# A rational feed-forward layer behind masked attention: the second matrix multiplication wholly in float16 parts, steps of 2048 columns, weights decoded two tiles at once, and another order of the last batch

## The chip, the cores and the metric

The kernel runs on one core of one Trainium2 chip. The metric is device time in microseconds (us), the median of the runs. A core has a matrix engine (TensorE, PE in the profile, with its weight loads as PEld), a vector engine (VectorE, DVE), a scalar engine (ScalarE, ACT), GpSimd (POOL) and a queue engine (SyncE, SP). Each runs its own instructions in the order in which they stand in the program, and they wait for each other by semaphores. GpSimd also issues many of the transfers, so its queue holds both arithmetic and transfers.

## The reference

Attention over 8 batches, 8 heads, 576 positions and 64 dimensions per head, in which only scores within `tau` of the row's maximum count. Its output, 4608 rows of 512, goes through a layer with 2048 hidden units, whose non-linearity is a ratio of polynomials:

```python
scores = scale * np.matmul(q, k.transpose(0, 1, 3, 2))
thresh = np.max(scores, axis=-1, keepdims=True) - tau
scores = np.where(scores >= thresh, scores, -1000000000.0)
scores = scores - np.max(scores, axis=-1, keepdims=True)
attn = np.exp(scores)
attn = attn / (np.sum(attn, axis=-1, keepdims=True) + 1e-09)
x = np.matmul(attn, v)                       # heads side by side: (4608, 512)
h = x @ w_in                                 # (512, 2048)
h2 = h * h
h3 = h2 * h
P = a[0] + a[1] * h + a[2] * h2 + a[3] * h3
Q = 1.0 + np.abs(b[0]) * np.abs(h) + np.abs(b[1]) * h2
g = P / (Q + 1e-06)
out = g @ w_out                              # (2048, 512)
```

The weights come as 64-bit words and are decoded to float32 on the chip.

## The kernel before

**Attention.** A unit is one pair of heads and one block of 128 query rows (four blocks and a rest of 64 rows; 160 units). Its scores go to three PSUM banks (L811 and L815; L804 for a rest), VectorE takes the maxima (L821, L823), ScalarE applies threshold and exponential (L836, L840), and the probabilities are split into a high float16 part, `hi` (L324 on ScalarE or L326 on VectorE), and a low one, which VectorE computes in L862 as probability times factor minus high part. A transfer transposes them and L933 multiplies them by V. The first batch goes another way, with transposes on TensorE (L885, L890, L916).

**The layer.** A chunk is 256 rows of x; there are 18 (two per batch, and two that gather the rests of four batches). The hidden units are 16 blocks of 128, called f. A step of the layer takes one chunk and four f, that is 1024 columns of a tile with 128 partitions. Per step:

- the first multiplication, L1050, in three float16 products (high by high, low by high, high by low), 12 multiplications of 256 columns for each f;
- ScalarE brings the result to a tile `t` (L1059);
- the ratio: |h| (L1064 on ScalarE or L1066 on VectorE), then on VectorE L1070, L1073, L1083, L1086, L1089 and L1092, each reading two inputs, with ScalarE's logarithm and exponential (L1077, L1080) in the middle for the reciprocal;
- the second multiplication by `w_out`. For three f of four (`PARTS`), g is split into a rounded part (L316 on ScalarE or L318 on VectorE, 256 columns each) and a remainder (L1100 on VectorE), both in the format fp32r, and L1109 makes three products of 512 columns. For the fourth f, L1113 multiplies in full float32, which the profile records as two instructions each;
- L1123 or L1118 takes the sum out of PSUM, and it is stored.

**Weights.** Each tile of 128 by 512 is loaded by GpSimd's queue, decoded by ScalarE and VectorE (L491, L497, L501, L331), and split. The scale of `w_in` comes from its largest absolute value (L543, L545 and `scale_ops`), four tiles at a time. GpSimd paces its loads with a small read of an earlier one (L481).

**The order.** No instruction is placed by hand. A planner, `Plan.order()`, simulates the engines while the program is built: every operation has a key (an aim in units of attention), a duration, what it waits for and which buffers it holds, and operations that two engines could do (`FLEX`) go to the one the planner finds sooner. The tables `WHEN`, `FLEX`, `START`, `PRICE` and `TOL` steer it. All batches go through the pairs of heads in one manner (`visits`): first half of the rows for three pairs, all rows of the fourth, then the second half and the rests on the way back. The last three chunks (`LAST`) come behind the last unit.

Of the kernel before, what the change touches and what calls it, by code (L numbers as in the profile page):

```python
# [26 lines left out]
POOLS = {"e": 3, "hi": 2, "pT": 2, "st": 8, "sc": 2, "t": 8, "u": 3, "g": 2, "x": 3, "xr": 1}  # L27
# [16 lines left out]
LAST = (0, 1, 2)
SOON = 1

# [10 lines left out]
PARTS = 3  # L57

# [27 lines left out]

TOL = {"PE": 0.1187, "ACT": 0.1137, "DVE": 0.0398, "POOL": 0.1, "DMA": 0, "GD": 0}
# [30 lines left out]
class Plan:  # L118
# [156 lines left out]
def masked_attention_rational_ffn(  # L275
# [54 lines left out]
    def tensor_tensor(dst, x, y, how):  # L330
# [28 lines left out]
    ones = bass.AP(one.tensor, one.offset, [list(one.ap[0]), [0, P]])  # L359

# [47 lines left out]
    co = op("DVE", 2.1, 6.0, monic, [co])  # L408

    def scale_ops(key, get, up, inv, s, after, ahead=0.0):  # L410
# [20 lines left out]
        def f3():  # L431
            p2 = box["p2"]
            nc.vector.tensor_reduce(box["m2"], box["all"], AX.X, ALU.max)
            nc.vector.tensor_single_scalar(p2.bitcast(I32), box["m2"].bitcast(I32), 0x7F800000, ALU.bitwise_and)
# [8 lines left out]
        return op("DVE", 0.68, key, f3, [o], (), [h, hb])  # L443
# [22 lines left out]
    def decode_ops(i, key, load, hold, dst=None):  # L466
# [4 lines left out]
        ht = Hold("u", 1)  # L471

        def ld():
# [8 lines left out]
            box["rw"] = load()  # L482
            loaded.append((box["rw"], plan.now))

        def f1():


            box["w"] = place(ht)
            w, words_ = box["w"], box["rw"][:, :, 1].bitcast(F32)
            if plan.eng == "ACT":  # L490
                nc.scalar.activation(w, words_, AF.Prelu, scale=REBIAS, alpha=SIGN)  # L491
# [11 lines left out]
        def f6():  # L503
            t = box["w"].bitcast(I32)
            if dst is None:
                tensor_tensor(box["rw"][:, :, 1], t, box["rw"][:, :, 0], ALU.add)
                box["w"] = box["rw"][:, :, 1].bitcast(F32)
            else:
                tensor_tensor(dst.bitcast(I32), t, box["rw"][:, :, 0], ALU.add)

        l = op("GD", 2.5, key - 2.0, ld, (), [hold])
        if i < NC:
            first_loads.append(l)
        o1 = op(FLEX["f1"], 0, key, f1, [l], [ht])
        o2 = op("ACT", 0.568, key, f2, [l])
        o4 = op("DVE", 0.335, key, f4, [o1])
        o6 = op(FLEX["f6"], 0, key, f6, [o4, o2], (), [ht] if dst is None else [ht, hold])
        return o6, box

# [4 lines left out]
    wm = const.tile([P, NW * NC], F32, name="wm")  # L524
# [771 lines left out]
```

## Time and profile before

| | |
|---|---|
| median of three runs | 1289.99 us (1289.88 to 1293.14) |
| profiled execution, span from first to last instruction | 1287.8 us |
| its own time with what lies around the span | not recorded apart; the fastest run is 2.1 us above the span |
| TensorE busy | 1254.2 us, 97% |
| VectorE busy | 1210.6 us, 94% |
| ScalarE busy | 1072.6 us, 83% |
| GpSimd busy | 229.4 us, 18% |
| mean granted TensorE clock | 0.995 |

Busy time is the union of an engine's instructions. On VectorE an independent successor begins some 0.08 us before its predecessor's recorded end, so what an instruction adds is the distance between two starts. On TensorE the chain of work that ended last shows what a group of multiplications takes.

### The profile page before, as it was taken

What the parts mean: (1) busy time and instruction counts of PE and PEld (TensorE: products, weight loads), DVE (VectorE), ACT (ScalarE), POOL (GpSimd) and SP (SyncE); (2) the same over time, 40 slices, a digit from 0 to 9 for tenths busy, and PEclk for the clock granted to TensorE, in tenths of its full rate; (3) what the DMA queues carried; (4) which work ended last, traced back from release to release, by engine and by line L of the source; (5) the groups of instructions that cost most, each with busy time, mean ns of one, the idle gap of its engine ahead of it and who ended that gap; (6) DMA issues with size and microseconds to landing.
All of it is one profiled execution on the core that took longest, in us unless ns stands there. A gap on an engine that the chain in (4) does not pass through costs nothing.

```text
span 1287.8 us, 25167 instructions
## 1 busy us (share of the span) xinstructions
PE 1254.2 (97%) x9296; PEld 899.3 (70%) x9296; DVE 1210.6 (94%) x1970; ACT 1072.6 (83%) x2166; POOL 229.4 (18%) x478
## 2 busy tenths in 40 slices
PE   8898999999999999999999999999999999999998
PEld 6666677677667776766777676677677677677775
DVE  5999899999999999999999999999999999998876
ACT  6988899899988888888888798888887988885454
POOL 2201000123122321232112231322122220200000
PEclk8999999999999999999999999999999999999999
DMA  8544355588567654878644775776566745542000
GB/s 243 159 124 142 117 98 102 111 149 168 93 121 142 132 111 100 124 139 122 110 86 102 130 139 108 154 130 139 94 116 132 135 101 96 110 96 29 17 17 17
DMA packets 338123, 146.64 MB, mean 114 GB/s; under 512 B 314416, under 2 KB 320720, under 8 KB 338000
## 3 DMA queue, kind: packets, MB, share of 16 engines
q1 hardware_dynamic: 316240, 87.14, 39.3%
q0 software_dynamic: 21440, 57.30, 16.5%
q8 instruction: 73, 1.20, 0.4%
q10 hardware_dynamic: 320, 0.59, 0.2%
q14 instruction: 50, 0.41, 0.1%
HBM read 60.30 MB, written 9.44 MB: 54 GB/s over the span
## 4 chain that ended last, share of the span: by engine, by line
PE 62%; DVE 17%; ACT 3%; issue 3%; DMA 2%; POOL 0%; DVEq 0%; ACTq 0%
PE banks L1050 20%; PE banks L1109 18%; PE banks L1113 8%; PE banks L815 7%; PE banks L933 7%; DVE e L862 3%; PE banks L804 2%; PE banks L811 2%; DVE t L1086 2%; DVE st L821 1%; DVE t L1092 1%; DVE t L1073 1%; DVE t L1089 1%; DVE t L1070 1%; DVE t L1083 1%
## 5 line engine op out<-in xcount | busy, mean ns | idle before, releaser
L1050 PEld LDWEIGHTS <-wi 128*128 128x128 f16 x3456 | 326.0, 98 | 104.8 <-issue 69.0
L1050 PE MATMUL banks<-x,wi 128*128 128x256 f16 x3072 | 363.6, 273 | 2.7 <-ACT t L1059 1.3
L1109 PE MATMUL banks<-wp,g 128*128 128x512 f32 x1296 | 357.6, 418 | 2.6 <-ACT g L316 1.7
L1109 PEld LDWEIGHTS banks<-wp,g 128*128 128x128 f32 x1296 | 235.7, 188 | 101.5 <-issue 36.8
L840 ACT ACTIVATE e<-e,cf 128x576 f32<-128x576 f32 x288 | 221.5, 775 | 0.4
L836 ACT ACTIVATE e<-banks,st 128x576 f32<-128x576 f32 x288 | 206.6, 737 | 14.7 <-DVE st L830 11.3
L862 DVE SCALAR_TENSOR_TENSOR e<-e,st,hi 128x576 f16<-128x576 f32 x252 | 205.0, 813 | 2.9 <-ACT hi L324 2.7
L821 DVE TENSOR_REDUCE st<-banks 128x2 f32<-128x1152 f32 x128 | 172.5, 1348 | 8.4 <-PE banks L815 8.0
L324 ACT ACTIVATE hi<-e,st 128x576 f16<-128x576 f32 x162 | 122.1, 770 | 47.4 <-DVE st L851 39.6
L1113 PE MATMUL banks<-wp,t 128*128 128x512 f32 x288 | 143.6, 613 | 2.8 <-DVE t L1092 2.8
L815 PE MATMUL banks<-KK,QQ 64*128 64x512 f32 x512 | 145.9, 645 | 0.0
L1059 ACT ACTIVATE t<-banks,hsc 128x512 f32<-128x512 f32 (+1 forms) x192 | 106.7, 575 | 36.3 <-PE banks L1050 35.4
L933 PEld LDWEIGHTS <-V 128*64 128x64 f16 x2520 | 104.2, 111 | 33.7 <-issue 30.5
L933 PE MATMUL banks<-pT,V 128*64 128x256 f16 (+1 forms) x2520 | 118.9, 248 | 3.8 <-DMA pT<-e 3.1
L1086 DVE SCALAR_TENSOR_TENSOR t<-t,co,t 128x1024 f32<-128x1024 f32 (+1 forms) x73 | 92.3, 1266 | 19.8 <-ACT t L1080 19.7
L316 ACT CAST g<-t 128x256 fp32r<-128x256 f32 x152 | 57.9, 402 | 45.7 <-PE banks L1109 34.7
L1077 ACT ACTIVATE t<-t,co 128x1024 f32<-128x1024 f32 (+1 forms) x73 | 82.7, 1133 | 12.8 <-DVE t L1083 12.4
L1092 DVE SCALAR_TENSOR_TENSOR t<-t,co,t 128x1024 f32<-128x1024 f32 (+1 forms) x73 | 92.4, 1266 | 0.6
L1083 DVE SCALAR_TENSOR_TENSOR t<-t,co,t 128x1024 f32<-128x1024 f32 (+1 forms) x73 | 92.4, 1266 | 0.0
L1070 DVE SCALAR_TENSOR_TENSOR t<-t,co 128x1024 f32<-128x1024 f32 (+1 forms) x73 | 92.3, 1264 | 0.0
L1073 DVE SCALAR_TENSOR_TENSOR t<-t,co 128x1024 f32<-128x1024 f32 (+1 forms) x73 | 92.3, 1264 | 0.0
L1089 DVE SCALAR_TENSOR_TENSOR t<-t,t 128x1024 f32<-128x1024 f32 (+1 forms) x73 | 88.0, 1206 | 0.7
(135 smaller groups left out, 1567.4 us busy)
## 6 DMA issues: line engine op xcount, KB each, us to landing
KK<-in_kT_dram POOLq DMA_DIRECT2D x84, 144.0 KB, 3.9
t<-in_w_in_dram POOLq DMA_DIRECT2D x16, 512.0 KB, 4.7
t<-in_w_out_dram POOLq DMA_DIRECT2D x16, 512.0 KB, 4.7
out_dram<-u POOLq DMA_DIRECT2D x26, 256.0 KB, 3.2
V<-in_v_dram POOLq DMA_DIRECT2D x24, 256.0 KB, 4.6
QQ<-in_qT_dram POOLq DMA_DIRECT2D x42, 144.0 KB, 3.0
QQ<-in_qT_dram POOLq DMA_DIRECT2D x42, 128.0 KB, 3.4
KK<-in_kT_dram SPq DMA_DIRECT2D x24, 144.0 KB, 3.0
```

Of the source, the lines that this page charges most:

```text
L324: nc.scalar.activation(dst, src, AF.Identity, scale=factor)
L815: nc.tensor.matmul(d, QQ[r, t * P:(t + 1) * P], KK[r, REM:S], **one)
L821: nc.vector.tensor_reduce(box["st"][:, 0:2], box["both"], AX.X, ALU.max, negate=True)
L836: nc.scalar.activation(ev(hh), box["s"][hh], AF.Prelu, scale=SCALE, bias=box["st"][:, 2 + hh:3 + hh], alpha=STEEP)
L840: nc.scalar.activation(e, e, AF.Exp, scale=passes, accum_out=box["st"][:, 4 + hh:5 + hh])
L862: nc.vector.scalar_tensor_tensor(box["lo"][:, c], ev(hh), box["st"][:, 6 + hh:7 + hh], box["hi"][:, c], ALU.mult, ALU.subtract)
L933: nc.tensor.matmul(dst, V[:, c * P + head * D:c * P + (head + 1) * D], rhs, start=c == 0 and n == 0, stop=c == NT and n == 2)
L1050: nc.tensor.matmul(d, wi_tile(c, f0 + j, hl), x[:, c, :], start=c == 0 and n == 0, stop=c == NC - 1 and n == 2)
L1059: nc.scalar.activation(box["h3"][:, 2 * k:2 * k + 2, sl], psv[:, :, sl], AF.Identity, scale=hsc[:, b2, g:g + 1])
L1086: nc.vector.scalar_tensor_tensor(box["q"], box["q"], qc, box["i"], ALU.add, ALU.mult)
L1109: nc.tensor.matmul(acc[tt], fr(g[:, x]), fr(wo[f][y]), start=begins and j == n == 0, stop=ends and j == nb - 1 and n == 2)
L1113: nc.tensor.matmul(acc[tt], box["r"][:, o:o + P], wo[f], start=begins and j == 0, stop=ends and j == nb - 1)
```

## The change

1. **Second multiplication.** All 16 f are done in three float16 products (L1322 in the new file). `PARTS`, the fp32r parts and the full float32 products are gone, and so is the pool `g`. `w_out` is held as a high and a low float16 part, scaled by a power of two for each half of the f.
2. **A scale from norms.** For float16, g needs a scale. For each chunk x is squared in bfloat16 (L1107 or L1109), TensorE sums the squares over a column with a matrix of ones (L1114), VectorE takes the largest sum and a rough root (L1117, `root`), GpSimd works out a bound for |g| in seven small operations (`bound`), VectorE rounds it to a power of two (`floor_ops`) and GpSimd writes the two factors (`gain`, `first_gain`). The scale of `w_in` comes from column norms too (L591, L593, L603, L607), and V's from a sum of squares in place of its maximum.
3. **Tiles of 2048 columns.** A step takes eight f (`NB`). Its elementwise work goes in pieces of 1024 columns (`PIECE`), and in whole steps (up to 2048 columns) for steps behind the last unit. A piece's g has one rounding (L341 or L343) and one remainder (L1313) for all its f. The last chunk's steps are 8, 4, 2 and 2 f (`TAIL`).
4. **Weights two tiles at once.** Loads and decoding work on 128 by 1024, in place in a tile `t`; with half as many loads the planner's order holds no pacing read any more.
5. **The last batch** goes through its rests of 64 rows first, then the first and then the second half (`ENDING`), and the last three chunks follow in that order (`LAST = (2, 0, 1)`).
6. **The planner's numbers.** All keys are now in a table `K`, and `WHEN`, `FLEX`, `START`, `PRICE`, `TOL` and the spacings have other values; the pool `t` has 7 buffers of twice the size.

```diff
-POOLS = {"e": 3, "hi": 2, "pT": 2, "st": 8, "sc": 2, "t": 8, "u": 3, "g": 2, "x": 3, "xr": 1}
+POOLS = {"e": 3, "hi": 2, "pT": 2, "st": 8, "sc": 2, "t": 7, "u": 3, "dg": 2, "x": 3, "xr": 1}
-PARTS = 3
+NB = 8
+PIECE = 2
+TAIL = (8, 4, 2, 2)
-LAST = (0, 1, 2)
+LAST = (2, 0, 1)
-PRICE = {"ACT": 0.7389, "DVE": 2.6699}
+PRICE = {"ACT": 2.362, "DVE": 1.311}
...
+    ENDING = [[half, other, rest][i] for i in LAST]
+        if bb == B - 1:
+            visits += [(v0 + i, x) for x in ENDING for i in range(NP)]
...
+        def f_norm():
+            sq = place(hq).bitcast(BF16).rearrange("p (c t) -> p c t", c=NC)
+            for c in range(NC):
+                nc.tensor.matmul(bank(hb)[:, 0:CT], ones_, sq[:, c, :], start=c == 0, stop=c == NC - 1)
+        def f_root():
+            nc.vector.tensor_reduce(w[:, 0:1], bank(hb)[:, 0:CT], AX.X, ALU.max)
+            root(w[:, 1:2], w[:, 0:1])
+    def bound(w, x, sigma):
+        m, k, p, q, hi = (w[:, i:i + 1] for i in range(2, 7))
+        g = nc.gpsimd
+        g.tensor_scalar(hi, w[:, 1:2], x, sigma, ALU.mult, ALU.mult)
+        g.tensor_scalar(m, hi, rqc, rbc, ALU.mult, ALU.min)
+        g.tensor_scalar(k, m, hi, 1.0, ALU.mult, ALU.min)
+        g.tensor_scalar(p, hi, g2, k, ALU.add, ALU.mult)
+        g.tensor_scalar(q, m, g1, g0, ALU.mult, ALU.add)
+        g.tensor_tensor(p, p, q, ALU.add)
+        g.tensor_scalar(p, p, 2.0 ** -100, 2.0 ** 100, ALU.max, ALU.min)
+    def floor_ops(w, key, after):
+            nc.vector.tensor_single_scalar(p.bitcast(I32), p.bitcast(I32), 0x7F800000, ALU.bitwise_and)
+            nc.vector.reciprocal(q, p)
...
+        span = nb // 2 if late else min(PIECE, nb // 2)
+        pieces = [(k, min(k + span, nb // 2)) for k in range(0, nb // 2, span)]
...
-        def f_gh(j):
-            copy(fr(box["g", j][:, 0]), box["r"][:, j * CT:(j + 1) * CT])
-        def f_gl(j):
-            nc.vector.tensor_tensor(fr(g[:, 1]), box["r"][:, j * CT:(j + 1) * CT], g[:, 0], ALU.subtract)
+        def f_gh(x):
+            times(g_parts(x)[0], cols("r", x), gscale)
+        def f_gl(x):
+            gh, gl = g_parts(x)
+            nc.vector.scalar_tensor_tensor(gl, cols("r", x), gscale, gh, ALU.mult, ALU.subtract)
         def f_g2(j, tt):
-            if in_parts(f):
-                for n, (x, y) in enumerate(((0, 0), (1, 0), (0, 1))):
-                    nc.tensor.matmul(acc[tt], fr(g[:, x]), fr(wo[f][y]), start=begins and j == n == 0,
-                                     stop=ends and j == nb - 1 and n == 2)
-                return
-            nc.tensor.matmul(acc[tt], box["r"][:, o:o + P], wo[f], start=begins and j == 0, stop=ends and j == nb - 1)
+            for n, (x, y) in enumerate(((0, 0), (1, 0), (0, 1))):
+                nc.tensor.matmul(acc[tt], g[x][:, o:o + P], wo_tile(f, y), start=begins and j == n == 0,
+                                 stop=ends and j == nb - 1 and n == 2)
```

**TensorE, second multiplication of one step.** `g`, `t` and `wp` are buffers, x2 counts repeats. Before, the end of a step in the last part of the program, one float32 block and the first of three fp32r blocks:

```order
L1113 MATMUL banks<-wp_154,t_70 128x512 x2
L1109 MATMUL banks<-wp_0_155,g_97 128x512 x2
L1109 MATMUL banks<-wp_1_156,g_97 128x512
L1109 MATMUL banks<-wp_0_155,g_97 128x512 x2
L1109 MATMUL banks<-wp_1_156,g_97 128x512
```

After, in float16, where the weight loads are instructions of their own:

```order
L1248 MATMUL banks<-x_97,wi 128x256
L1322 LDWEIGHTS t_68
L1322 MATMUL banks<-wp_134,t_68 128x512
L1322 LDWEIGHTS t_68
L1322 MATMUL banks<-wp_134,t_68 128x512
L1322 LDWEIGHTS t_68
L1322 MATMUL banks<-wp_134,t_68 128x512
```

One kind of product stands where two stood. Behind the scores of the last unit stand 480 of the first layer's multiplications (L1050), 216 of L1109 and 24 of L1113 before; after, 396 of L1248 and 330 of L1322, with eight of L1114.

**VectorE, in the middle of the program.** Before, with the ratio (L1070 to L1092), the remainders of g at 256 columns (L1100) and attention's low parts (L862):

```order
L1092 SCALAR_TENSOR_TENSOR t_74<-t_74,co,t_75 128x1024
L851 RECIPROCAL st_92<-st_92 128x2
L823 TENSOR_REDUCE st_93<-banks 128x1
L1100 TENSOR_TENSOR g_97<-t_74,g_97 128x256
L1100 TENSOR_TENSOR g_96<-t_74,g_96 128x256
L830 TENSOR_SCALAR st_93<-st_93,cf 128x1
L1070 SCALAR_TENSOR_TENSOR t_73<-t_68,co 128x1024
L862 SCALAR_TENSOR_TENSOR e_81<-e_81,st_92,hi_83 128x576
L1073 SCALAR_TENSOR_TENSOR t_72<-t_72,co 128x1024
L862 SCALAR_TENSOR_TENSOR e_81<-e_81,st_92,hi_83 128x576
L1100 TENSOR_TENSOR g_97<-t_74,g_97 128x256
```

After, at about the same place (L1273, L1277, L1287, L1291, L1295 and L1299 are the ratio, L932 the low parts):

```order
L1291 SCALAR_TENSOR_TENSOR t_72<-t_72,co,t_69 128x1024
L891 TENSOR_REDUCE st_91<-banks 128x2
L921 RECIPROCAL st_90<-st_90 128x2
L1295 SCALAR_TENSOR_TENSOR t_72<-t_72,t_69 128x1024
L1287 SCALAR_TENSOR_TENSOR t_71<-t_71,co,t_68 128x1024
L1299 SCALAR_TENSOR_TENSOR t_73<-t_73,co,t_72 128x1024
L932 SCALAR_TENSOR_TENSOR e_82<-e_82,st_90,hi_84 128x576
L1277 SCALAR_TENSOR_TENSOR t_70<-t_70,co 128x1024
L1313 SCALAR_TENSOR_TENSOR t_72<-t_73,gsc,t_72 128x1024
L932 SCALAR_TENSOR_TENSOR e_82<-e_82,st_90,hi_84 128x576
```

One remainder of 1024 columns (L1313) stands for three of 256, and two pieces of one step run through the ratio side by side (`t_71`, `t_72`). Over the whole program VectorE's roundings of `hi` go from 90 to 32 and ScalarE's from 162 to 220.

**GpSimd's queue, in the middle.** Before, loads of K and Q and stores follow each other:

```order
L653 DMA KK_116<-in_kT_dram 64x576
L654 DMA KK_116<-in_kT_dram 64x576
L718 MEMSET V_163 64x64 x2
L1132 DMA out_dram<-u_78 128x512
L1132 DMA out_dram<-u_76 128x512
L690 DMA V_161<-in_v_dram 128x4x128
```

After, a chunk's bound and factors (`gt`, `gsc`, `oscs` are columns of single numbers) stand between a store and the next load of Q:

```order
L1345 DMA out_dram<-u_77 128x512
L1130 TENSOR_SCALAR gt<-gt,isx,sg 128x1
L1131 TENSOR_SCALAR gt<-gt,co 128x1
L1132 TENSOR_SCALAR gt<-gt 128x1
L1133 TENSOR_SCALAR gt<-gt,co 128x1
L1134 TENSOR_SCALAR gt<-gt,co 128x1
L1135 TENSOR_TENSOR gt<-gt 128x1
L1136 TENSOR_SCALAR gt<-gt 128x1
L1176 TENSOR_SCALAR gsc<-gs,gt 128x2
L1177 TENSOR_SCALAR oscs<-gt,sg 128x1
L714 DMA QQ_115<-in_qT_dram 64x576
```

Over the program 186 such small operations are new on GpSimd, and the 11 pacing reads of L481 are gone.

More of the change, by code (lines that the diff above doesn't have):

```diff
@@ L141, in op @@
         engs = {eng: dur} if isinstance(eng, str) else eng
-        o = Op(engs, key, fn, [x for x in after if x is not None], list(take), list(drop))
+        o = Op(engs, key + self.shift, fn, [x for x in after if x is not None], list(take), list(drop))
         o.rank, o.tiling = self.rank, "ff"
@@ L504, in f6, with squares_ops, f @@
             t = box["w"].bitcast(I32)
-            if dst is None:
-                tensor_tensor(box["rw"][:, :, 1], t, box["rw"][:, :, 0], ALU.add)
-                box["w"] = box["rw"][:, :, 1].bitcast(F32)
-            else:
[L509 to L518, printed above, removed]
+            if dst is not None:
+                box["w"] = dst
+            tensor_tensor(box["w"].bitcast(I32), t, low.bitcast(I32), ALU.add)
+        l = op("GD", 3.4, key - 2.0 + K["load"], ld, (), [hold])
+        if i < NC // 2:
+            first_loads.append(l)
+        o1 = op(FLEX["f1"], 0, key + K["f1"], f1, [l])
+        o2 = op("ACT", 0.995, key + K["f2"], f2, [l])
+        o4 = op("DVE", 0.6, key + K["f4"], f4, [o1])
+        o6 = op(FLEX["f6"], 0, key + K["f6"], f6, [o4, o2], (), [hold])
+        return o6, box
+    def squares_ops(key, box, acc, after, take, drop, junk):
+        def f():
+            if plan.eng == "ACT":
+                nc.scalar.activation(junk(), box["w"], AF.Square, accum_out=acc)
+            else:
+                nc.vector.scalar_tensor_tensor(junk(), box["w"], 1.0, box["w"], ALU.mult, ALU.mult, accum_out=acc)
+        return op(FLEX["junk"], 0, key + K["junk"], f, after, take, drop)
     def w_key(i, j):
@@ L614, in masked_attention_rational_ffn @@
     end = x0
+    begin_ = [min(pos[bb * NP + i, t] for i in range(NP) for t in range(NT + 1)) for bb in range(B)]
     VW = NT * P + 2 * D
@@ L1165, in moe_ops @@
[L1165 to L1170 removed]
+                h = op("ACT", 0.58 if kind == "m" else 0.25, p + 0.4 * k + K["h"], lambda k=k, i=i: f_h(k, i),
+                       [l1[k], h] + [hsc_done[b][(f0 + 2 * k) // NC] for b in hs] + [co], [hh] if (k, i) == (0, 0) else (), [bhs[k]])
@@ new lines, in moe_ops, with on @@
+            hk.append(h)
+        piece_of, gl_of = {}, {}
+        p1 = p
+        for x in pieces:
+            p = p1 + 0.4 * x[1] - 0.4
+            h = hk[x[1] - 1]
+            t0 = x[0] == 0
+            def on(f, x=x):
+                return lambda: f(x)
+            A = op(can(act(0.156), dve(0.074, 1.92)), 0, p + K["A"], on(f_A), [h], [hq] if t0 else ())
+            r2 = op("DVE", dve(0.105), p + K["r2"], on(f_r2), [h], [hr] if t0 else ())
+            q = op("DVE", dve(0.105), p + K["q"], on(f_q), [A])
+            r3 = op("DVE", dve(0.105), p + K["r3"], on(f_r3), [r2])
+            ln = op("ACT", act(0.205), p + K["ln"], on(f_ln), [q, r3])
+            iv = op("ACT", act(0.136), p + K["inv"], on(f_inv), [ln])
+            e = op("DVE", dve(0.105), p + K["e"], on(f_e), [iv])
+            nn = op("DVE", dve(0.074), p + K["n"], on(f_n), [e], (), [hh])
+            gd = op("DVE", dve(0.105), p + K["g"], on(f_g), [nn, r3])
+            gh = op(can(act(0.17), dve(0.127, 1.92)), 0, p + K["gh"], on(f_gh), [gd, gsc_done[ck, fh if first else 0]])
+            gl = op("DVE", dve(0.129), p + K["gl"], on(f_gl), [gh], (), [hr])
+            for j in range(2 * x[0], 2 * x[1]):
+                piece_of[j], gl_of[j] = x, gl
@@ L1187, in moe_ops @@
             through = f0 + nb == NF
-            part = Hold("t", 2)
+            if not through and not parts:
+                parts["hold"], parts["by"] = Hold("t", 4), None
             for tt in range(2):
```

543 lines of the change are left out of this document (339 added, 204 removed), and 4 rows, old and new, of the table K.

## The prediction

> **What bounds the kernel now.** I read the page's first part, the stretches, the chain that ended last, the groups by form, the waits and the timelines, in this order. Busy time comes first:
>
> ```profile
> PE 1254.2 (97%) x9296; PEld 899.3 (70%) x9296; DVE 1210.6 (94%) x1970; ACT 1072.6 (83%) x2166; POOL 229.4 (18%) x478
> ```
>
> Two engines are nearly full, so the stretches decide which of them paces where. A row holds PE, PEld, DVE, ACT and POOL:
>
> ```profile
> 0.00:200.00 200.00, 183.98 (x1317) 136.05 (x1318) 173.60 (x393) 171.13 (x361) 27.20 (x73) 0.97 0.53 148
> 200.00:1150.00 950.00, 938.72 (x7114) 663.81 (x7113) 929.33 (x1444) 828.12 (x1673) 201.65 (x404) 1.00 0.64 120
> 1150.00:1287.80 137.80, 131.49 (x872) 99.44 (x868) 107.69 (x135) 73.39 (x134) 0.55 (x1) 1.00 0.12 25
> 200.00:250.00 50.00, 50.00 (x382) 36.42 (x379) 50.00 (x72) 43.71 (x83) 0.00 (x0) 1.00 0.45 89
> 450.00:500.00 50.00, 50.00 (x346) 35.14 (x345) 49.96 (x71) 44.13 (x86) 8.36 (x16) 1.00 0.52 108
> ```
>
> The reader is to see three stages. In the middle one, from 200 to 1150 us, TensorE and VectorE are both full: VectorE is idle for 950 - 929.3 = 20.7 us of 950, and in good stretches for 0 and 0.04 of 50. In the first it is idle for 26.4 us, in the last for 30.1, and there TensorE alone paces. Idle time of VectorE is thus 77.2 us, and 1210.6 + 77.2 is the span, 1287.8. A saving on TensorE is worth its full size in the last stage only. In the middle it is worth what VectorE stops waiting. So I make the sum on VectorE: its busy time after the change, and its idle time by stage.
>
> **TensorE's part.** The chain gives the price of a group in a full stretch (start, length, group):
>
> ```profile
> 480.07 1.81 PE banks L1113 x4
> 481.88 2.80 PE banks L1109 x12
> ...
> 487.56 3.29 PE banks L1050 x30
> ```
>
> One fp32r product of 512 columns takes 2.80 / 12 = 0.233 us, one full float32 multiplication (two records) 0.905, a float16 product of 256 columns 0.110. A float16 product of 512 columns doesn't occur. It is bounded by 2 x 0.110 = 0.219 and by the fp32r row, 0.233, of the same columns; I take 0.219, since the row of 256 columns has the same type. Counts stand in the groups:
>
> ```profile
> L1109 PE MATMUL banks<-wp,g 128*128 128x512 f32 x1296 | 357.6, 418 | 2.6 <-ACT g L316 1.7 <-DVE g L1100 0.9
> L1113 PE MATMUL banks<-wp,t 128*128 128x512 f32 x288 | 143.6, 613 | 2.8 <-DVE t L1092 2.8
> ```
>
> Before: 1296 x 0.233 + 144 x 0.905 = 432 us. After: 1728 x 0.219 = 378 (403 by the upper bound). Added are 72 sums of squares at 0.110 and 16 of 512 columns at 0.219, 11 us, and some 3 us of eight more warm-up multiplications. Net: 40 us less, to 1214 (16 less by the upper bound). TensorE falls below VectorE.
>
> **VectorE's part.** Starts in the timeline give what an instruction adds:
>
> ```profile
> 1157.16 0.52 DVE L326 TENSOR_SCALAR hi<-e,st 128x576 f16<-128x576 f32 x1
> 1157.59 0.81 DVE L862 SCALAR_TENSOR_TENSOR e<-e,st,hi 128x576 f16<-128x576 f32 x1
> ...
> 1171.67 1.28 DVE L1073 SCALAR_TENSOR_TENSOR t<-t,co 128x1024 f32<-128x1024 f32 x1
> 1172.87 0.75 DVE L1100 TENSOR_TENSOR g<-t,g 128x256 fp32r<-128x256 f32 x2
> 1173.54 1.28 DVE L1083 SCALAR_TENSOR_TENSOR t<-t,co,t 128x1024 f32<-128x1024 f32 x1
> ```
>
> A two-input operation takes 1.20 us at 1024 columns and 0.335 at 256; on that line 0.62 at 512 and 2.35 at 2048. A one-input rounding of 576 takes 0.43.
>
> - Remainders of g: 216 x 0.335 = 72.4 go; 63 of 1024, four of 2048 and two of 512 come, 75.6 + 9.4 + 1.2 = 86.2. That is +13.8, since a fourth of the f had no remainder. The ratio's six lines: 6 x (71 x 1.20 + 2 x 0.62) = 518.6 become 6 x 86.2 = 517.2, -1.4.
> - Roundings of g and of attention's `hi`, which the planner deals out anew:
>
> ```profile
> L318 DVE CAST g<-t 128x256 fp32r<-128x256 f32 x64 | 18.1, 292 | 4.5 <-PE banks L1109 4.0
> L316 ACT CAST g<-t 128x256 fp32r<-128x256 f32 x152 | 57.9, 402 | 45.7 <-PE banks L1109 34.7 <-DVE t L1092 10.3
> L326 DVE TENSOR_SCALAR hi<-e,st 128x576 f16<-128x576 f32 x90 | 45.8, 518 | 0.5
> L324 ACT ACTIVATE hi<-e,st 128x576 f16<-128x576 f32 x162 | 122.1, 770 | 47.4 <-DVE st L851 39.6 <-DMA pT<-hi 3.3 <-issue 2.5
> L1066 DVE TENSOR_SCALAR t<-t 128x1024 int32<-128x1024 int32 x13 | 8.9, 688 | 0.4 <-ACT t L1059 0.3
> L1064 ACT ACTIVATE t<-t 128x1024 f32<-128x1024 f32 x58 | 61.1, 1054 | 0.7
> ```
>
>  For g, 64 x (0.292 - 0.08), 13 us, become 24 of mostly 1024 columns. Their price lies between 0.60 (L1066, 0.688 - 0.08) and 0.76 (L326 by columns); at 0.66 it is 16: +3. Of `hi`, 58 go to ScalarE: -58 x 0.43 = -25.
> - Weights. The decoding's parts have these rows:
>
> ```profile
> L331 DVE CUSTOM_DVE_ANT_0 t<-t,u 128x1024 uint16<-128x1024 uint16 x28 | 19.3, 690 | 0.7 <-ACT st L828 0.2
> L501 DVE TENSOR_SCALAR u<-u 128x512 int32<-128x512 int32 x32 | 13.5, 424 | 2.9 <-ACT u L491 2.9
> L561 DVE SCALAR_TENSOR_TENSOR wi<-t,sw,wi 128x512 f16<-128x512 f32 x16 | 11.3, 747 | 0.0
> L591 DVE TENSOR_TENSOR wp<-t,wp 128x512 fp32r<-128x512 f32 x12 | 8.2, 687 | 0.1
> ```
>
>  Half as many of twice the length save only the fixed part: about 1 us each on L331, L501 and L561. The low parts of `w_out` go from 12 x 0.60 to 8 x 1.20, +2.4; squares, maxima, high parts and copies from some 16 to 24. Together +7.
> - Norms. A chunk's maximum over 256 columns of PSUM costs about 0.34, like L945 below, and its four one-column operations 0.1 each; 18 chunks make 13.5 us. Nine squares of x at 0.6 (L1066) add 5.4, the set-up 1: +20.
>
> ```profile
> L945 DVE TENSOR_SCALAR x<-banks 128x256 f16<-128x256 f32 x4 | 1.7, 421 | 1.7 <-PE banks L933 1.6
> L434 DVE TENSOR_SCALAR sc<-sc 128x1 int32<-128x1 int32 x12 | 1.8, 154 | 0.4
> ```
>
> - Fewer small operations (PSUM evictions, thresholds, |h|) go to ScalarE: -6.
>
> The sum is 13.8 - 1.4 + 3 - 25 + 7 + 20 - 6 = +11, so VectorE is busy for 1222 us. ScalarE gains 58 x 0.67 = 39 us of `hi` (0.77 less some 0.1 of overlap), nine squares at 0.95, 9, and 5 of evictions, while the roundings of g stay near 45. It comes to 1126 us.
>
> **Idle time of VectorE by stage.** First stage: 26, as before. The layer starts later, behind the scores of 17 units where it was 12, but both orders reach the same work on TensorE by the 25th unit. Bounds: 18 (fewer, larger loads) and 38 (the extra work of this stage, 11 us by the order, not hidden). Middle: 20.7 us was the price of TensorE being full. With 40 us less there it tends to what full stretches show, 0 to 0.04 per 50 us, or 1 in 950; ScalarE at 91% gives some of it back. I take 8, between 1 and 20.7, nearer the full stretches. Last stage: TensorE paces. One step of four f takes 11.17 us there:
>
> ```profile
> 1204.93 4.45 PE L1109 MATMUL banks<-wp,g 128*128 128x512 f32 x18
> ...
> 1216.10 4.45 PE L1109 MATMUL banks<-wp,g 128*128 128x512 f32 x18
> ```
>
> By the order, what stands behind the last unit's scores costs 480 x 0.110 + 216 x 0.233 + 24 x 0.905 = 125 us before and 396 x 0.110 + 330 x 0.219 + 1 = 117 after. So the stage shrinks from 137.8 to about 130 us. VectorE has 7 us more in it, 115 in all, and idles for 15. The whole steps of 2048 columns lengthen a step's chain of waits, but the first multiplication runs two steps ahead of the second in the order, some 20 us each, which covers it; without that cover a step would wait for nine operations of 2048 columns in a row, each some 1.1 us longer, 10 us a step.
>
> Span: 1222 + 26 + 8 + 15 = 1271 us, or 1.3% less. The fastest run shown is 2.1 us above the profiled span, the median 2.2; with 2, rounded, I predict 1273 against 1289.99. TensorE at 1214 then is 57 us idle, so it is not the bound.
>
> Transfers: the loads of K and Q cost nothing, because their cover is the second buffer:
>
> ```profile
> POOL QQ L646 <- PE banks L815: 167.5, 16, 15.8
> ```
>
> GpSimd waits 167.5 us for TensorE to free a buffer here, not the other way about. Loads stand behind a chunk's nine small operations now; at some 0.2 us each they are 2 us later, within those waits. Were they not, the scores would be late and VectorE's maxima (L821) with them.
>
> **Rivals.** *More is gained.* If the start loses its decoding stalls (18) and the middle reaches 3, the span is 1222 + 18 + 3 + 10 = 1253, some 1255 in all. For it speaks that half the load instructions go; against it, that a later start leaves TensorE nothing to do.
>
> *ScalarE takes TensorE's place.* VectorE's waits for ScalarE are there already:
>
> ```profile
> DVE t L1086 <- ACT t L1080: 19.7, 12, 2.3
> DVE e L862 <- ACT hi L324: 2.7, 1, 2.7
> ```
>
> With 58 more `hi` on ScalarE, L862's successor waits on its queue more often. If the middle stays at 20.7 us, the time is 1286; if L1086's 19.7 comes once more, 1306. I give no change up to 1294, slower above. Against it: ScalarE still has 9% free.
>
> *GpSimd blocks VectorE* (the other side). In the weights' stage a pacing read of GpSimd met VectorE, and later one did not:
>
> ```profile
> 38.58 0.69 POOL L481 TENSOR_SCALAR cf<-t 1x1 f32<-1x1 f32 x1
> 42.74 0.18 POOL L481 TENSOR_SCALAR cf<-t 1x1 f32<-1x1 f32 x1 [1.66 <-DMA t<-in_w_in_dram]
> ...
> 38.53 0.69 DVE L591 TENSOR_TENSOR wp<-t,wp 128x512 fp32r<-128x512 f32 x1
> ```
>
> The read took 0.69 us instead of 0.18, while VectorE kept its usual 0.69 (group mean 687 ns). If each of the 186 new operations cost VectorE their full 0.18 us, that is 33 us, and the time 1306; from (1294 - 1273) / 186 = 0.11 us each the kernel is slower. The rows show GpSimd as the one that waits, so I give it little. [...]
>
> *The products aren't cheaper.* At 0.233 the stage behind the last unit grows by 330 x 0.014 = 5 us, to 1278; this lies in the forecast's own range.
>
> **How the numbers follow.** The forecast, 1273 with 1260 to 1285 as its own range, has 0.48; more gained (1245 to 1260) 0.18; ScalarE 0.24 (0.02 faster, 0.13 no change, 0.09 slower); GpSimd 0.10 (all but 0.01 slower). No change means within 0.3%, 1286 to 1294, about what a measurement can tell. Faster: 0.48 + 0.18 + 0.02 = 0.68; same 0.14; slower 0.18. The range from 1253 to 1298 leaves out the ends of the rivals, under 2 in 10.
>
> **What would show it.** Right: L1322 at about 0.219 us in the chain, VectorE busy near 1222 us and idle for under 10 us per 950 in the middle, TensorE near 1214 us, the stage behind the last unit near 130 us. Wrong: VectorE's waits for ScalarE over 40 us; L1313 or the ratio's lines longer than 1.28 us where GpSimd works; a first stage with over 38 us of idle VectorE; TensorE waiting for L1313 in the last steps.

## The result: 1341.7 us, 4% slower

The changed kernel took 1341.68 us (median of four runs, 1340.87 to 1342.67), the kernel before 1289.93 beside it: a ratio of 1.040, 95% interval 1.0385 to 1.0417. Predicted were 1273 and a range from 1253 to 1298. The experiments find two losses behind the difference, and in both it is VectorE's waiting that grew, hardly its work: the chain that computes the scale of g stops VectorE 18 times and ScalarE 9 times, some 58 us, and the weight loads of the first 13 us delay K and V, some 10 us. With both taken away (the scale a constant) the time was 1278. A version that computes the scale once for a batch, far ahead, and holds the loads back took 1273.9 us, 1.5% less than the kernel before beside it (1292.5).

### The profile page after: what moved, and what is told of

Its sections match the earlier page's. It is cut to its first block, busy times and chain, and to the rows that moved or that the text cites. A ratio compares the mean times of both kernels' runs of the same rounds, so it can differ in the third digit from the quotient of the medians.

```text
span 1340.9 us, 25552 instructions
## 1 busy us (share of the span) xinstructions
PE 1236.1 (92%) x9540; PEld 802.3 (60%) x9540; DVE 1220.4 (91%) x1789; ACT 1112.9 (83%) x2111; POOL 336.6 (25%) x663
## 3 DMA queue, kind: packets, MB, share of 16 engines
q0 software_dynamic: 22304, 60.25, 16.2%
## 4 chain that ended last, share of the span: by engine, by line
DVE 27%; PE 18%; ACT 7%; issue 6%; POOL 4%; DMA 3%; POOLq 0%; DVEq 0%; ACTq 0%
PE banks L1322 9%; DVE e L932 5%; PE banks L1248 5%; DVE st L891 4%; DVE t L1313 2%; DVE t L1299 2%; DVE t L1273 2%; DVE t L1291 2%; DMA pT<-e 2%; PE banks L1003 2%; DVE t L1287 2%; DVE t L1277 2%; PE banks L885 2%; DVE t L1295 1%; ACT e L906 1%
## 5 line engine op out<-in xcount | busy, mean ns | idle before, releaser
L1322 PE MATMUL banks<-wp,t 128*128 128x512 f16 x1728 | 408.8, 385 | 21.2 <-DVE t L1313 12.1
L1248 PEld LDWEIGHTS <-wi 128*128 128x128 f16 x3456 | 333.3, 98 | 116.6 <-issue 61.1
L1248 PE MATMUL banks<-x,wi 128*128 128x256 f16 x3072 | 366.3, 274 | 13.3 <-ACT t L1258 11.2
L1322 PEld LDWEIGHTS <-t 128*128 128x128 f16 x1728 | 163.5, 99 | 241.5 <-issue 45.9
L906 ACT ACTIVATE e<-banks,st 128x576 f32<-128x576 f32 x288 | 208.4, 734 | 24.0 <-DVE st L900 16.0
L932 DVE SCALAR_TENSOR_TENSOR e<-e,st,hi 128x576 f16<-128x576 f32 x252 | 204.6, 812 | 3.3 <-ACT hi L341 2.8
L891 DVE TENSOR_REDUCE st<-banks 128x2 f32<-128x1152 f32 x128 | 172.6, 1348 | 23.1 <-PE banks L885 22.9
L341 ACT ACTIVATE hi<-e,st 128x576 f16<-128x576 f32 x220 | 166.9, 766 | 23.7 <-DVE st L921 18.2
L885 PE MATMUL banks<-KK,QQ 64*128 64x512 f32 x512 | 150.3, 665 | 0.0
L1003 PEld LDWEIGHTS <-V 128*64 128x64 f16 x2520 | 104.9, 111 | 31.8 <-issue 26.4
L1280 ACT ACTIVATE t<-t,co 128x1024 f32<-128x1024 f32 (+2 forms) x69 | 81.4, 1180 | 23.9 <-DVE t L1287 23.4
L1291 DVE SCALAR_TENSOR_TENSOR t<-t,co,t 128x1024 f32<-128x1024 f32 (+2 forms) x69 | 91.3, 1324 | 8.2 <-ACT t L1283 8.2
L714 POOL DMA_DIRECT2D QQ<-in_qT_dram x47 | 26.0, 554 | 288.9 <-PE banks L885 155.3
L1313 DVE SCALAR_TENSOR_TENSOR t<-t,gsc,t 128x1024 f16<-128x1024 f32 (+2 forms) x69 | 91.4, 1325 | 5.5 <-ACT t L341 5.4
L1299 DVE SCALAR_TENSOR_TENSOR t<-t,co,t 128x1024 f32<-128x1024 f32 (+2 forms) x69 | 91.3, 1324 | 0.1
L1277 DVE SCALAR_TENSOR_TENSOR t<-t,co 128x1024 f32<-128x1024 f32 (+2 forms) x69 | 91.4, 1324 | 0.0
L1273 DVE SCALAR_TENSOR_TENSOR t<-t,co 128x1024 f32<-128x1024 f32 (+2 forms) x69 | 91.4, 1324 | 0.0
L1287 DVE SCALAR_TENSOR_TENSOR t<-t,co,t 128x1024 f32<-128x1024 f32 (+2 forms) x69 | 91.3, 1323 | 0.1
L341 ACT ACTIVATE t<-t,gsc 128x1024 f16<-128x1024 f32 (+2 forms) x45 | 53.6, 1192 | 45.2 <-POOL gsc L1176 25.5
```

Of the source, the lines that this page charges most:

```text
L341: nc.scalar.activation(dst, src, AF.Identity, scale=factor)
L885: nc.tensor.matmul(d, QQ[r, t * P:(t + 1) * P], KK[r, REM:S], **one)
L891: nc.vector.tensor_reduce(box["st"][:, 0:2], box["both"], AX.X, ALU.max, negate=True)
L906: nc.scalar.activation(ev(hh), box["s"][hh], AF.Prelu, scale=SCALE, bias=box["st"][:, 2 + hh:3 + hh], alpha=STEEP)
L932: nc.vector.scalar_tensor_tensor(box["lo"][:, c], ev(hh), box["st"][:, 6 + hh:7 + hh], box["hi"][:, c], ALU.mult, ALU.subtract)
L1003: nc.tensor.matmul(dst, V[:, c * P + head * D:c * P + (head + 1) * D], rhs, start=c == 0 and n == 0, stop=c == NT and n == 2)
```

## The profile after

The page's busy times, then the stretches (PE, PEld, DVE, ACT, POOL; behind them the granted TensorE clock):

```profile
PE 1236.1 (92%) x9540; PEld 802.3 (60%) x9540; DVE 1220.4 (91%) x1789; ACT 1112.9 (83%) x2111; POOL 336.6 (25%) x663
```

```profile
0.00:200.00 200.00, 163.38 (x1087) 113.70 (x1088) 155.70 (x339) 154.49 (x290) 25.97 (x66) 0.89 0.39 127
200.00:1150.00 950.00, 900.02 (x7274) 579.51 (x7273) 906.15 (x1296) 846.37 (x1643) 276.58 (x547) 0.98 0.63 121
1150.00:1340.90 190.90, 172.74 (x1184) 109.07 (x1181) 158.54 (x155) 112.05 (x180) 34.02 (x50) 0.97 0.25 49
```

VectorE is busy for 1220.4 us; the sum said 1222. But it is idle for 44.3, 43.9 and 32.4 us in the three stages, 120.5 in all, where the sum said 26, 8 and 15. No engine is full in the middle stage any more (VectorE 906.2 us of 950, TensorE 900.0). The list of waits names what VectorE stood before (total, times, longest):

```profile
DVE gt L1141 <- POOL gt L1136: 35.0, 18, 3.7
DVE st L891 <- PE banks L885: 22.9, 11, 8.0
DVE u L771 <- DMA V<-in_v_dram: 5.8, 1, 5.8
```

L1141 is the first operation of `floor_ops`, L1136 the last of `bound`. What waited for the factor that follows is in the answer on the tile `gsc`:

```profile
ACT t L341: 31.0, 9
```

L341 is the rounding of g. GpSimd's side of it, from the groups (the mean ns of one stands behind the busy time), and one chunk in the timelines of GpSimd, VectorE and TensorE; behind them the same stretch with its granted clock (the last column but two), and an L1322 of the chain of work that ended last:

```profile
L1130 POOL TENSOR_SCALAR gt<-gt,isx,sg 128x1 f32<-128x1 f32 x18 | 22.3, 1236 | 105.6 <-DVE gt L453 98.6 <-DVE st L900 3.5 <-DVE st L917 2.7
L1176 POOL TENSOR_SCALAR gsc<-gs,gt 128x2 f32<-128x2 f32 x16 | 19.2, 1198 | 6.2 <-DVE gt L1142 5.9 <-POOL V L787 0.2
L1131 POOL TENSOR_SCALAR gt<-gt,co 128x1 f32<-128x1 f32 x20 | 13.2, 661 | 2.1
```

```profile
465.55 0.55 POOL L1345 DMA_DIRECT2D out_dram<-u  x1
466.19 0.33 POOL L1130 TENSOR_SCALAR gt<-gt,isx,sg 128x1 f32<-128x1 f32 x1
...
468.51 0.22 POOL L1136 TENSOR_SCALAR gt<-gt 128x1 f32<-128x1 f32 x1
469.21 1.69 POOL L1176 TENSOR_SCALAR gsc<-gs,gt 128x2 f32<-128x2 f32 x1 [0.49 <-DVE gt L1142]
```

```profile
463.73 1.35 DVE L891 TENSOR_REDUCE st<-banks 128x2 f32<-128x1152 f32 x1
468.76 0.15 DVE L1141 TENSOR_SCALAR gt<-gt 128x1 int32<-128x1 int32 x1 [3.68 <-POOL gt L1136]
469.22 1.21 DVE L1295 SCALAR_TENSOR_TENSOR t<-t,t 128x1024 f32<-128x1024 f32 x1
```

```profile
471.83 0.80 PE L881 MATMUL banks<-KK,QQ 128*128 128x128 f32 x2 [4.05 <-ACT e L906]
474.57 1.46 PE L1322 MATMUL banks<-wp,t 128*128 128x512 f16 x3
475.82 0.63 PE L474 MATMUL banks<-u,cf 128*128 128x128 f32 x2
```

```profile
470.00:476.00 6.00, 4.17 (x10) 1.80 (x11) 5.92 (x9) 5.14 (x13) 2.17 (x4) 0.62 0.53 104
```

```profile
1207.35 0.65 PE banks L1322 x3
```

From 465.1 to 468.8 VectorE does nothing but wait: until 466.2 GpSimd still issues a store that stands before the bound in its queue, and then come seven operations on one column. What VectorE owes attention (a threshold, L900) comes late, so ScalarE's L906 comes late, and TensorE stands for 4.05 us. By the starts, three products of L1322 then take 475.82 - 474.57 = 1.25 us, 0.42 each, where three of that line take 0.65 in the chain elsewhere; the granted clock of the stretch is 0.62, and 0.50 from 474.6 to 476. The mean granted clock of the execution is 0.968, before 0.995. So the stretch behind this stall was slow as well; how much of the lost time is lost clock, no run separates.

From the start of L1130 to the end of L1136 I read 2.53 to 4.91 us over the 20 bounds, 3.76 on the average, and 1.68 on the average for the two outputs, L1176 and L1177. The planner believes 1.6 and 0.4.

## The experiments

Each kernel keeps the changed kernel's order of work where nothing else is said.

**1. A constant scale** (`e1_const`).

```diff
     def bound(w, x, sigma):
+        return
...
-        return op("DVE", 0.15, key, f, [after])
+        return op("DVE", 0.15, key, lambda: None, [after])
```

> Leaves out the computed scale: the bound's seven GpSimd operations and VectorE's two operations behind them are not issued, the scale is a constant, and every other instruction stands where it stood. Theory A (the chain through GpSimd stops VectorE and ScalarE): the 35.0 us of VectorE's waits for the bound and the 31.0 us of ScalarE's waits for its output go; the second partly hides behind the first, so 35 to 60 us off 1341.7, about 1295 us. Theory B (the waits only show a lateness that is there anyway, in the order or in the start and the last batch; other waits take their place): over 1325 us.

Measured: 1283.8 us (ratio to the kernel before 0.9959, 0.9942 to 0.9977). Page and stretches:

```profile
PE 1217.8 (95%) x9540; PEld 796.2 (62%) x9540; DVE 1213.6 (95%) x1751; ACT 1111.2 (87%) x2111; POOL 279.5 (22%) x523
```

```profile
0.00:200.00 200.00, 167.03 (x1144) 117.20 (x1145) 160.40 (x345) 159.93 (x300) 19.51 (x52) 0.91 0.43 133
200.00:1150.00 950.00, 926.64 (x7574) 601.45 (x7572) 942.51 (x1321) 884.08 (x1729) 243.72 (x465) 1.00 0.66 125
1150.00:1281.20 131.20, 124.09 (x828) 77.58 (x825) 110.70 (x87) 67.24 (x83) 16.25 (x6) 1.00 0.13 29
```

58 us less, of which only 6.8 us are VectorE's work: theory A. In the middle VectorE is idle for 950 - 942.5 = 7.5 us, and TensorE keeps its clock there (1.00, against 0.98 in the changed kernel).

**2. The bound twice** (`e2_twice`).

```diff
+        for _ in range(2):
             g.tensor_scalar(hi, w[:, 1:2], x, sigma, ALU.mult, ALU.mult)
...
```

> The bound is computed twice over on GpSimd, 140 operations more, on an engine that is busy for a quarter of the span. Theory A: one bound takes about 3.8 us (2.5 to 4.9) and 18 of the 20 have no room behind them, so 18 x 3.1 to 3.8 = 56 to 68 us more, about 1405 us, and VectorE's wait for the bound grows from 35 to 90 us or more. Theory B: GpSimd has room, under 1355 us.

Measured: 1398.5 us, 56.8 more.

```profile
DVE gt L1141 <- POOL gt L1136: 81.9, 18, 5.8
```

A bound takes 6.61 us on the average, 2.85 more; times 20 that is 57. What the bound takes longer comes back in full in the time, though GpSimd is idle for nearly three quarters of the span (busy for 383.3 us of 1397.6).

**3. The bound on VectorE** (`e5_on_dve`).

```diff
-        g = nc.gpsimd
+        g = nc.vector
```

The other small operations in `first_gain` and `gain` likewise.

> The same operations of the bound and of its output, all issued by VectorE at the places where they stood in the order of work, GpSimd has none of them. VectorE gets some 180 operations of 128x1 at 0.154 us and 0.03 us between, 33 us more work. Theory A: both waits, worth 35 to 60 us, go and 33 come in their place: 1315 to 1340 us, about 1328. Theory B: nothing is gained by the waits and the work is added, 1370 us or more.

Measured: 1337.0 us. VectorE's busy time is 1252.5 us, 32.1 more, as expected, but with the time only 4.7 us lower, 36.8 us of waiting went, where the constant scale took away 57.9 - 6.8 = 51. VectorE's wait at L1141 is gone; ScalarE's L341 still stands 17.6 us before `gsc`. It is no repair: the work costs nearly what the wait did.

**4. The same rules, another order** (`c1_control`) and **5. that order with the constant scale** (`e9_control_const`).

```diff
-        o = op("POOL", 1.6, key, f, [norm_done[ck], ready_all])
+        o = op("POOL", 1.61, key, f, [norm_done[ck], ready_all])
```

The price in `first_gain` likewise.

> Only the planner's price of the bound is changed, from 1.60 to 1.61 us: the same work in another order from the same rules. Theory A (a chain of real length 3.8 us and another 1.7 us that the planner takes for 1.6 and 0.4): the stall comes with every such order, 1335 to 1355 us. Theory C (the kernel's constants fit one order alone, and the new kernel's order is just a bad one): a change of more than 15 us in either direction.

> The control's order of work (bound priced at 1.61) with the constant scale of the first run, so the computed scale is left out there too. If the stall by the bound costs the same in every order: 1363.4 less 58 makes 1305 us, 1298 to 1315, and the other 22 us are the order's own. If the 58 us belonged to the one order that the kernel's constants were made for: over 1330 us.

Measured: 1363.4 and 1312.6 us. So an order drawn anew costs 21.7 us with the stall and 28.8 without it, more than the 15 that I allowed, and theory C holds for that much. The stall costs 51 us in this order and 58 in the other: it comes with both, and what the new order costs is added to it. In experiments 1 to 3, which keep the changed kernel's order, the order plays no part.

**6. The planner told the truth** (`e3_priced`).

```diff
-        o = op("POOL", 1.6, key, f, [norm_done[ck], ready_all])
-        return op("POOL", 0.4, key, f_out, [floor_ops(w, key, o)])
+        o = op("POOL", 5.0, key, f, [norm_done[ck], ready_all])
+        return op("POOL", 2.0, key, f_out, [floor_ops(w, key, o)])
```

> The planner is told 5.0 us for the bound and 2.0 us for its output in place of 1.6 and 0.4, and orders all work anew. Theory A: VectorE's wait for the bound falls from 35 us to under 8 and ScalarE's for its output from 31 to under 8; with the 22 us that a mere new order cost in the control, 1363 less about 55 makes 1308 us, 1285 to 1325. Theory C (the order decides, not the wait): over 1345 us although both waits are gone.

Measured: 1341.1 us, a miss.

```profile
DVE gt L1141 <- POOL gt L1136: 9.7, 10, 2.3
```

The wait fell from 35 to 9.7 us and ScalarE's before `gsc` from 31 to 7.6, but the time is 33 us above the expected 1308, in the new order. Something is learnt from the bound's own length: it grew from 3.76 to 5.68 us on the average, as would follow if VectorE now works beside it (experiment 11). VectorE is busy for 9.9 us more in this order and still idle for 107 us, and ScalarE's longest wait is now for the ratio (L1280 for L1287, 41.1 us against 23.4 in the changed kernel). What makes this order lose its time I did not settle.

**7. Two weight loads at a time** (`e6_two_loads`).

```diff
-AHEAD = 3
+AHEAD = 2
```

In the changed kernel no pacing read stands among the first seven loads of 1024 KB, because the planner takes 3.4 us for each, where it took 2.5 for half of it, and so finds the third one back 10.2 us old, past its limit of 9 (`RECENT`). GpSimd's timeline:

```profile
7.69 3.09 POOL L584 DMA_DIRECT2D t<-in_w_in_dram  x4 [0.36 <-issue]
10.79 2.13 POOL L634 DMA_DIRECT2D t<-in_w_out_dram  x3
```

All seven are out by 12.9 us. The second V is issued from 18.6 us on and ScalarE gets it at 38.5:

```profile
38.53 0.74 ACT L774 ACTIVATE u<-V 128x640 bf16<-128x640 f32 x1 [11.32 <-DMA V<-in_v_dram]
```

> Only the first weight loads: a load of 1024 KB is issued once the load two before it has landed, not three before within 9 us of planned time; nine small GpSimd operations more, all other orders unchanged. Theory D (in the first 60 us seven loads of 1024 KB go out together and the loads of K, Q and V land behind them, so that ScalarE and VectorE stand before V for 11.3 and 5.8 us and TensorE behind them): VectorE's idle time in the first 200 us falls from 44.3 towards the 26.4 of the kernel before, 10 to 20 us off 1341.7, about 1327 us. Rival: the weights then come too late for their decoding, and the time stays within 4 us of 1341.7 or grows.

Measured: 1332.2 us, 9.5 less. The same line, and the first stage:

```profile
28.75 0.74 ACT L774 ACTIVATE u<-V 128x640 bf16<-128x640 f32 x1 [2.81 <-DMA V<-in_v_dram]
```

```profile
0.00:200.00 200.00, 168.55 (x1170) 118.97 (x1170) 163.70 (x352) 162.75 (x307) 31.37 (x77) 0.92 0.45 134
```

VectorE's idle time in the stage falls from 44.3 to 36.3 us. This bears out theory D, though just below its range of 10 to 20: the 8 us fit the 9.5. The loads of K in the first 60 us land 9.1 us after their issue in the changed kernel (median of six), 6.5 here and 5.9 in the kernel before; the median for the five loads of V does not show it (2.9, 7.6 and 5.2), only ScalarE's wait for the second one does.

**8. Both taken away** (`e7_const_two_loads`).

> The two edits that each took a wait away, together: the constant scale (the computed one is left out) and weight loads held to two at a time. If they are two separate losses: 1283.8 less 9.5 makes 1274 us, 1270 to 1280, which is the sum that the prediction made. If the loss at the start is part of the same stall: 1282 to 1287.

Measured: 1278.0 us (1271.2 to 1280.2); ratio 0.987, 0.983 to 0.990. The losses add up, nearly.

**9. A repair that failed** (`b1_batch`). V's scale bounds every probability-weighted mean of V, so six times it is a bound on the norms, without any sums. `f` is a chunk's bound, `rest` what VectorE and the outputs do behind it, and `count` counts VectorE's operations; both chunks of a batch come at once:

```diff
+    nc.vector.memset(gt[:, :, 1:2], 6.0 * 2.0 ** 14)
...
-        o = op(FLEX["sqx"], 0, key + K["sqx"], f_sqx, x_done[ck], [hq], [xh_hold[ck]])
+        o = op(FLEX["sqx"], 0, key + K["sqx"], lambda: None, x_done[ck], [hq], [xh_hold[ck]])
...
+                f, *rest = early.pop(ck)
+                f()
+                soon_.append((count + 12, *rest))
```

> The norms are not computed: a bound on them that holds for every batch (six times the scale of V that the kernel already has) takes their place, so the squares, the 72 sums on TensorE and VectorE's 18 maxima with their roots go, and the GpSimd operations and VectorE's two behind them are issued as soon as the batch's scale of V stands, twelve VectorE operations apart, far ahead of their use. All else stands in the order of the changed kernel. Theory A: the gain of the run with a constant scale (58 us) is kept, and VectorE's busy time is 1220.4 less 7.5, 2.8, 2.8, 4.8 and 1.4 us, so some 13 us under that run: about 1271 us, 1262 to 1280. Theory B (a bound on GpSimd stalls VectorE wherever it stands): over 1300 us.

Measured: 1321.7 us, 50 above the expected.

```profile
DVE gt L1143 <- POOL gt L1137: 20.5, 10, 3.1
```

Twelve operations were too few for two bounds, and GpSimd itself stood 41.8 us before V's scale (L447), with the loads of K and Q behind it in its queue; how the 50 us divide between the two was not tried. With two loads at a time (`b2_both`):

> Both edits: no norms, the scale of a batch computed ahead, and weight loads held to two at a time. Theories A and D together: 1271 less 10 to 20, about 1257 us, below both kernels. If the start is hidden behind something else: the same as the run without the norms.

1312.1 us: 9.6 less than without that edit, as in experiment 7, and still above the kernel before.

**10. The scale far ahead** (`b3_ahead`). One bound for a batch, 20 VectorE operations behind V's scale, the rest another 40 later, and two loads at a time.

```diff
+                d1, d2 = (2, 10) if k[0] == "first" else (20, 60)
+                jobs += [(count + d1, [f]), (count + d2, [g] + [x for y in outs for x in y])]
...
-AHEAD = 3
+AHEAD = 2
```

> The scale computed once for a batch from the bound on the norms, on GpSimd, 20 VectorE operations after the batch's scale of V stands, VectorE's two operations and the outputs another 40 later; no norms; two loads at a time. If the run without norms lost its gain because two bounds stood back to back in front of GpSimd's loads and VectorE came to them after 12 operations (it waited 20.5 us for them): no wait for the bound over 2 us in all, and 1274 less the 19 us of work that the norms took from VectorE, plus 4 for the operations that come back, about 1260 us, 1250 to 1272. If the order of work suffers from any operation that leaves it: over 1290 us.

Measured: 1273.9 us (1270.5 to 1277.9); ratio 0.9855, 0.9828 to 0.9881, so it beats both kernels. It is 14 above the expected. Four of these stood already in experiment 8. Against that experiment VectorE's work falls by 12.6 us, not by 15, and its idle time grows by 3.4. The other 5 are the spread between executions: the profiled one lies 3.3 us under its median here and 2.1 above it there.

```profile
0.00:200.00 200.00, 173.12 (x1239) 122.49 (x1240) 170.03 (x360) 168.50 (x319) 42.33 (x86) 0.96 0.48 139
200.00:1150.00 950.00, 924.38 (x7517) 597.76 (x7515) 933.81 (x1284) 879.50 (x1726) 300.73 (x520) 0.99 0.64 125
1150.00:1268.70 118.70, 111.87 (x717) 68.75 (x715) 97.66 (x67) 54.59 (x59) 1.11 (x2) 0.99 0.08 23
```

VectorE waits for a bound only once here, 1.0 us, and is idle for 16.2 us in the middle; its longest waits over the program are for TensorE (L891, 13.4 us) and ScalarE (L1301, 11.8 us).

**11. What holds GpSimd up** (`e8_bound_alone`): forty bounds behind the last step.

```diff
+    for times_, other_ in beside:
...
+        for _ in range(10):
+            bound(gt[:, 0, :], isx[:, 0:1], sg[:, 0:1])
+        for _ in range(times_):
+            other_()
```

> The changed kernel with forty bounds more behind its last step, read in the trace alone: ten with VectorE idle, ten beside VectorE operations with two float32 inputs of 128x1024, ten beside operations with one float32 input, ten beside two float16 inputs. If VectorE's operations hold GpSimd up: about 2.5 us for one bound with VectorE idle, as the shortest in the kernel, and 4 to 9 us beside two inputs. If GpSimd's operations merely take that long: the same 3.8 us in all four, and so with VectorE idle.

Timelines of GpSimd with VectorE idle, and of GpSimd and VectorE beside two-input operations:

```profile
1343.00 0.38 POOL L1131 TENSOR_SCALAR gt<-gt,co 128x1 f32<-128x1 f32 x1
...
1344.88 0.22 POOL L1136 TENSOR_SCALAR gt<-gt 128x1 f32<-128x1 f32 x1
1345.17 0.34 POOL L1130 TENSOR_SCALAR gt<-gt,isx,sg 128x1 f32<-128x1 f32 x1
```

```profile
1391.82 1.32 POOL L1130 TENSOR_SCALAR gt<-gt,isx,sg 128x1 f32<-128x1 f32 x1
1393.24 1.22 POOL L1131 TENSOR_SCALAR gt<-gt,co 128x1 f32<-128x1 f32 x1
...
1400.73 1.32 POOL L1130 TENSOR_SCALAR gt<-gt,isx,sg 128x1 f32<-128x1 f32 x1
```

```profile
1384.05 7.62 DVE L1498 SCALAR_TENSOR_TENSOR t<-t,t 128x1024 f32<-128x1024 f32 x6
```

One bound takes 2.54 us alone (from 1342.56, the start of its L1130, to 1345.10), 8.8 beside two-input operations of float32 or float16, and 5.85 beside one-input float32 operations. Two starts of L1130 are 8.91 us apart, seven operations, so 1.27 each, just the 7.62 / 6 of VectorE's: one GpSimd operation goes to one VectorE operation. (VectorE's own spacing here, 1.27 us, is not the kernel's 1.20. The operations of a set all write one tile; whether that or GpSimd beside them lengthens it, no run separates.) Beside the one-input operations (five in 3.65 us, 0.73 each) the starts are 5.93 us apart, eight of them for seven.

## Why the prediction was wrong, point by point

VectorE's idle time by stage, in us (span less busy time):

| | to 200 us | to 1150 us | rest | sum |
|---|---|---|---|---|
| before | 26.4 | 20.7 | 30.1 | 77.2 |
| predicted | 26 | 8 | 15 | 49 |
| after | 44.3 | 43.9 | 32.4 | 120.5 |
| constant scale | 39.6 | 7.5 | 20.5 | 67.6 |
| and two loads | 30.9 | 12.5 | 20.5 | 63.8 |

The last row in the profile:

```profile
0.00:200.00 200.00, 173.77 (x1231) 123.10 (x1232) 169.12 (x360) 168.70 (x315) 27.65 (x66) 0.94 0.46 137
200.00:1150.00 950.00, 921.98 (x7513) 598.08 (x7511) 937.55 (x1310) 877.68 (x1721) 241.67 (x460) 1.00 0.66 125
1150.00:1277.90 127.90, 120.81 (x801) 74.98 (x799) 107.41 (x83) 64.41 (x77) 16.25 (x6) 1.00 0.13 29
```

- *VectorE's work, 1222 us:* right, 1220.4. ScalarE's 1126 was 1112.9.
- *Products at 0.219 us:* right; the chain has 0.65 us for three of L1322, 0.217 each. *TensorE at 1214:* 1236.1, but 1216.6 once the stalls are gone, which fits the mean clock of 0.968 against 0.988 there.
- *Middle stage, 8 us:* the step that failed. It was what the stage can do without the chain (7.5, or 12.5 with two loads as well), and the chain was left out of it. I priced the "nine small operations" at "some 0.2 us each" as a delay to the loads behind them, "within those waits". That was the wrong customer: VectorE's `floor_ops` and the rounding of g wait for them, in order, at every chunk. The size was wrong too: 3.76 and 1.68 us for the nine, not 2.
- *First stage, 26 us:* 44.3. Part 4 of the change said that no pacing read was left, and the bounds of 18 and 38 looked at the decoding alone. Two loads at a time brought it to 36.3; without the stalls by the bound as well, 30.9.
- *Last stage, 15 us idle in 130:* the window after 1150 us is 190.9 us long because everything before is late; it has 32.4 us idle. With the stalls gone it is 127.9 long, close to the 130 said, with 107 us of VectorE's work in it, not 115, and so 20.5 idle. The rests first and the steps of 2048 columns were not tested apart.
- *Loads of K and Q covered by the second buffer:* right for the middle of the program, where GpSimd still waits 155.3 us for TensorE (L714 for L885); wrong at the start, where K and V came behind the weights (K 9.1 us after its issue, before 5.9; ScalarE stood 11.3 us before the second V).
- *"GpSimd blocks VectorE", 0.10:* the right engine, but half the price (33 us for 58) and the wrong mechanism. VectorE's operations did not get longer, they stood waiting for a result; the groups by form, of the changed kernel and of the one before:

```profile
L1273 DVE SCALAR_TENSOR_TENSOR t<-t,co 128x1024 f32<-128x1024 f32 x63 | 80.5, 1277 | 0.0
```

```profile
L1073 DVE SCALAR_TENSOR_TENSOR t<-t,co 128x1024 f32<-128x1024 f32 x71 | 90.8, 1279 | 0.0
```

  It is GpSimd that became slower: beside VectorE's 1.27 us operations one of its own came every 1.27 us, against 0.36 alone (experiment 11). That GpSimd slows VectorE likewise, no run here shows. In the changed kernel's timelines 28 of the two-input operations of 1024 columns have an operation of the chain beside them and the next VectorE operation right behind: none took over 1.28 us, and the next started 1.19 us later on the average, as behind 406 without one.
- *"ScalarE takes TensorE's place", 0.24:* not seen; VectorE's wait for ScalarE in the ratio (L1291) is 8.2 us, before 19.7, and all its waits for ScalarE 30, under the 40 named as a sign. Of the other signs, the first stage's 38 us was passed, and TensorE waits for L1313 12.1 us in 8 times.
- *The chances:* I had no case for a chain of dependent small operations across three engines, and I took GpSimd's shortest rows, 0.18 us, for its price; a bound alone, with nothing in its way, takes 2.54 / 7 = 0.36 for each operation.

## What to carry to other kernels

When a change adds a result that others wait for, follow it from the last engine that makes it to the first that needs it, and price the whole chain at the in-order queue of the consumer, however short each operation and however idle the engine in between. Whatever is needed once in a while should be made long before its use and from what stands early; here a looser bound, made once for a batch and long before its use, beat a tighter one at every chunk (1273.9 against 1332.2 us, both with two loads at a time); made twice for a batch, with VectorE's part only twelve operations behind, it took 1312.1. When an edit drops a pacing device as a side effect, price the traffic it held back.

## What the hardware showed that was not expected

GpSimd's small operations took 0.19 to 0.38 us alone, and beside VectorE's they came no faster than VectorE's own, of each kind tried: two float32 or float16 inputs (1.27 us between starts) or one float32 input (0.73 us). A chain of seven took 2.54 us alone, 8.8 beside the first two kinds and 5.85 beside the third; the 3.76 us of the changed kernel and the 5.68 of experiment 6 lie between. And TensorE lost clock behind a gap of 4.05 us: a granted clock of 0.50 and 0.42 us for a product behind it, 0.217 elsewhere. Whether the gap brought the lower clock about, no run tests.
